# Handing out a Fourier layer over fewer tiles of a dense loop, and moving its loads and stores between queues

## The chip, the cores and the metric

The kernel runs on one core of a Trainium2 chip. The metric is the device time of one run, in microseconds (us); less is better. The core has five engines, each of which takes its instructions in the order in which they were written out: PE (TensorE, matmuls), DVE (VectorE), ACT (ScalarE), POOL (GpSimdE) and SP (SyncE, which here only issues DMA transfers). POOL and ACT can issue DMA transfers too.

## The reference

A Fourier layer over 8 sequences of 3008 steps by 256, then a gated two-layer network over each of the 24,064 rows, all in float32:

```
X = rfft(x, axis=1)                                   # (8, 1505, 256)
Yr = Xr @ w_r - Xi @ w_i + b_r ;  Yi = Xr @ w_i + Xi @ w_r + b_i
Yr, Yi = softshrink(Yr, 0.01), softshrink(Yi, 0.01)
y = irfft(Yr + 1j * Yi, n=3008, axis=1)               # (8, 3008, 256)
h = y @ w_in                                          # 256 -> 2048, w_in in float64
out = (h * cos(h)) @ w_out                            # 2048 -> 256, w_out in float64
```

## The kernel before

**The work.** The transform of length 3008 is a two-dimensional one of 64 by 47. A batch goes through three stages. Stage A (`stage_a`, line 379) loads x in 12 pieces xt (line 387), takes the transform of length 64 in 6 bursts of matmuls (pa) and stores the result by ao to a scratch array scr1 (line 403). Stage B (`stage_b`, line 409) loads it again as at (line 429), takes the transform of length 47 (pb, line 467), mixes the channels with the complex weights (`wmix`, pw, lines 514 to 516), shrinks, and takes the inverse of length 47 (`inverse`, pi). It goes through a batch in four quarters q = 0 to 3 of 8 frequencies. Stage C (`stage_c`, line 671) loads the result as bt (line 679) and takes the last inverse (pc, line 687) for one tile of 512 rows (the sixth: 448), which gives the dense network's input as a high and a low part, xTh and xTl.

For batches 1 to 7 a quarter ends so: VectorE forms st (lines 525 to 538), GpSimdE folds it (line 551 to 563), VectorE transposes it into tr, SP stores tr to a scratch array scrT in two halves (line 569) and loads it back as y in four pieces (line 576). `spread` (line 579) then has PE read y (pi) and SP store the result by bo to scr2 (line 592), from which bt is loaded. In batch 0, which runs alone at the start, `idft` (line 619) does this with a store at line 631.

**The dense network.** For each tile `moe_step` (line 718) runs 16 times: six matmuls ph (lines 725 to 727), four steps on ACT and DVE for h cos h, its high half gh on ACT, its low half gl on GpSimdE for every second step (line 267, called at line 738) or on DVE (line 270), and, three steps later, six matmuls po (`second`, lines 707 to 711). The weights' float64 words come in 16 pieces (raw, line 217) that are split in the start.

**What sets the order.** Batch b's dense work goes together with stage B of batch b + 1 and stage A of batch b + 2: the stages are generators that yield a cost, and `ahead` (line 796) is pulled twice in a dense step, at a rate that `share` (line 820) sets. `share` divides the cost of a batch's Fourier work by 6 - SPREAD tiles for batches 1 to 7, and by 5 - SPREAD_FIRST for batch 0. `stage_b` yields 5.0 ahead of its last inverse (line 665), to give y time. After the Fourier work, `ahead` yields a gap (GAP) and then stage C's first tile of the next batch. From this the framework's scheduler makes the final order of each engine when the program is built, by its own model of the time. The input tiles xt and at share one ring of six buffers (`stage_in`, line 320), so each load waits until PE has read what its buffer held. bt has one buffer, y one.

Of the kernel before, what the change touches and what calls it, by code (L numbers as in the profile page):

```python
# [38 lines left out]
GAP = 7  # L39
A_EVERY, A_FIRST = 5, 13  # L40
A_PAIR = 1.15
SPREAD, SPREAD_FIRST = 1.2, 1.1


def _r11(a):
# [95 lines left out]
def tile_body(ctx: ExitStack, tc, x, w_r, w_i, b_r, b_i, w_in, w_out,  # L141
              c_f2, c_sig, c_f3, c_ff, c_if, c_iw, c_sgn, out):
    nc = tc.nc
# [128 lines left out]
    scr1, scr2 = {}, {}  # L272
# [25 lines left out]
    def two(name):  # L298

        if "pro" not in pool:  # L300
            return [fps(name) for _ in range(2)]
        p = [ps.tile([128, 512], F32, tag=f"o{h}", name=name, bufs=1) for h in range(2)]
        side.extend((q, []) for q in p)
        return p
# [3 lines left out]
    def burst(calls):  # L308

        with tc.issue_after(mark["fill"].ins) if "pro" in pool else ExitStack():  # L310
            ins = mm(*calls[0][0], **calls[0][1])  # L311
        kept, n = (side, 3) if "pro" in pool else (ring, 4)
        if len(kept) >= n:
            for r in kept[-n][1]:
                behind(ins, r, "bank")
        with tc.high_priority(), tc.issue_after(ins.ins):
            for a, k in calls[1:]:
                mm(*a, **k)

    def stage_in(name):  # L320
        return wk.tile([128, 512], F32, tag="xt", name=name, bufs=6)

    def stage_out(name):
        return wk.tile([128, 1024], F32, tag="ao", name=name, bufs=3)
# [54 lines left out]
    def stage_a(b):  # L379
        scr1[b] = dr.tile([32, 2, 2, 24, 256], F32, tag="scr1", name=f"scr1_{b}")  # L380
        ld = {}

        def load(c):
            if c < 12:
                ld[c] = stage_in("xt")
                with tc.issue_after(mark["f0", 2].ins) if b == 1 else ExitStack():
                    nc.sync.dma_start(ld[c], x[b, :, 512 * c:512 * (c + 1)])

        for c in range(2):
            load(c)  # L390
        yield 0.0
        yield 1.0
        for cc in range(6):
            p = two("pa")
            xs = [ld.pop(2 * cc + v) for v in range(2)]
            burst([((p[h][64 * v:64 * v + 64], ff[64 * h:64 * h + 64, 256:], xs[v][64 * h:64 * h + 64]),
                    dict(start=True, stop=True, skip_group_check=True)) for h in range(2) for v in (1, 0)])
            ao = stage_out("ao")
            for h in range(2):
                drained(p[h], nc.scalar.copy(ao[:, 512 * h:512 * h + 512], p[h]))  # L400
            for v in range(2):
                i = 4 * cc + 2 * v
                nc.sync.dma_start(scr1[b][:, :, :, i:i + 2].rearrange("s r g i d -> (s r) g (i d)"),
                                  ao[64 * v:64 * v + 64].rearrange("p (g x) -> p g x", g=2))
                load(2 * cc + 2 + v)
            yield A_PAIR


    def stage_b(b):
        scr2[b] = dr.tile([48, 2, 32, 256], F32, tag="scr2", name=f"scr2_{b}")  # L410
        ld = {}
# [184 lines left out]
        def inverse(q):  # L596
            if b:
                yield from spread(q)
                return
            st = ST.pop(q)  # L600

            def t2(j):
                p = fps("pt")
                for sl in range(2):
                    for e in range(2):
                        o = sl * 256 + e * 128
                        nc.tensor.transpose(p[:96, o:o + 128],
                                            st[:, e, 2 * j + sl].rearrange("p r k -> p (r k)"), ident)
                y = pool["pro"].tile([128, 512], F32, tag="yf", name="yf", bufs=2)[:96]
                for sl in range(2):  # L610
                    ds = slice(256 * sl, 256 * sl + 256)
                    sc = sig[:, 8 * q + 2 * j + sl:8 * q + 2 * j + sl + 1]
                    if sl:
                        nc.vector.tensor_scalar(out=y[:, ds], in0=p[:96, ds], scalar1=sc, scalar2=None, op0=ALU.mult)
                    else:
                        nc.scalar.activation(y[:, ds], p[:96, ds], AF.Copy, scale=sc)
                Y[j] = y

            def idft(j):
                p = fps("pi")  # L620
                parts = ((0, 256, 0), (256, 512, 1)) if (q == 0 and j == 0) else ((0, 512, 1),)
                y = Y.pop(j)
                for lo, hi, v in parts:
                    ins = mm(p[:96, lo:hi], fi[0][:, v], y[:, lo:hi], start=lo == 0, stop=hi == 512,
                             skip_group_check=True)
                if q < 3:
                    mark["fill"] = ins
                bo = stage_out("bo")[:96, :512]
                nc.scalar.copy(bo, p[:96])
                s0 = 8 * q + 2 * j  # L630
                nc.sync.dma_start(scr2[b][:, :, s0:s0 + 2].rearrange("n r s d -> (n r) (s d)"), bo)

            t2(0)
            yield 0.43
            for j in range(4):
                if j < 3:
                    t2(j + 1)
                    yield 0.43
                else:
                    yield 0.8  # L640
                idft(j)
                yield 0.65
# [28 lines left out]
    def stage_c(b, t):  # L671
        th = pool["mo"].tile([128, 2, 512], F32R, tag="xTh", name="xTh", bufs=2)
        tl = pool["mo"].tile([128, 2, 512], F32R, tag="xTl", name="xTl", bufs=2)
        xT[b, t] = (th, tl)

        bt = wk.tile([128, 4, 256], F32, tag="bt", name="bt", bufs=1)
        for g in range(2):
            n0 = 24 * g + 4 * t
            nc.sync.dma_start(bt[64 * g:64 * g + 64],
                              scr2[b][n0:n0 + 4].rearrange("i r s d -> (r s) i d"))  # L680
        yield 3.5
        for hf in range(2):
            p = fps("pc")
            for j in range(2):
                for c in range(2):
                    o = 256 * j + 128 * c
                    ins = mm(p[:, o:o + 128], bt[:, 2 * hf + j, 128 * c:128 * c + 128], ff[:, 128:256], start=o == 0, stop=o == 384,  # L687
                             skip_group_check=True)
            mark.setdefault("pc", ins.ins)
            pv = p.rearrange("p (j c n) -> p c j n", j=2, c=2)  # L690
            thv, tlv = (a[:, :, 256 * hf:256 * hf + 256].rearrange("p c (j n) -> p c j n", j=2) for a in (th, tl))
            nc.scalar.copy(thv, pv)
            drained(p, nc.vector.tensor_tensor(out=tlv, in0=pv, in1=thv.bitcast(F32), op=ALU.subtract))
        yield 1.72
# [94 lines left out]
    for _ in stage_c(0, 0):  # L789
        pass  # L790
# [36 lines left out]
    for b in range(NB):  # L827
        fa = ahead(b)
        for t in range(NTT):
# [20 lines left out]
            while open_[0]:  # L850
                c = next(fa, None)
# [30 lines left out]
```

## Time and profile before

| | us |
|---|---|
| three runs: lowest, median, highest | 2718.5, 2720.4, 2724.3 |
| the profiled execution | 2718.7 |
| its span (first to last instruction) | 2716.9 |
| PE, DVE, ACT, POOL busy | 2656, 1786, 1676, 990 |
| mean granted clock of TensorE | 0.993 of 2.4 GHz |

A row of the profile names the line of the kernel, the engine, and what an instruction writes and reads (out<-in). Idle time of an engine stands in front of the instruction that ended it, with what released it. SPq is SP's queue of DMA issues; a DMA piece runs from its issue until its data has landed. One matmul of the program with plain float32 operands appears as two records. Fourier work of batch b stands beside dense work of batch b - 1, so "batch 2" below means the Fourier work of batch 2, from about 442 us to 770 us.

### The profile page before, as it was taken

How to read it: one execution, taken by the hardware profiler on the slowest of the kernel's cores; microseconds unless marked ns; L12 is line 12 of the kernel's file. 1: busy time of each engine (PE TensorE's matmuls, PEld its weight loads, DVE VectorE, ACT ScalarE, POOL GpSimd, SP SyncE). 2: the span in 40 equal slices, each digit the busy share in tenths (PEclk: the TensorE clock that was granted, in tenths of full speed). 3: DMA queues.
4: the chain of work that ended last, by engine and by line, in shares of the span. 5: the costliest groups of instructions: out<-in, count | busy, mean ns of one | idle time of the engine just before them, and what ended most of it. 6: DMA issues, size and time to landing. Idle time of an engine off the chain costs nothing.

```text
span 2716.9 us, 36600 instructions
## 1 busy us (share of the span) xinstructions
PE 2655.9 (98%) x13161; PEld 2181.1 (80%) x13161; DVE 1785.8 (66%) x2856; ACT 1676.3 (62%) x3020; POOL 989.7 (36%) x907
## 2 busy tenths in 40 slices
PE   8789999999999999999999999999999999999999
PEld 6468778888788887888878877788787888888888
DVE  6577765676657666676666666667665677656665
ACT  5566566656566665666566566665665666666666
POOL 4345432344314442244322544234332344422222
PEclk9899999999999999999999999999999999999999
DMA  6332343134311443124331234312433022211000
GB/s 194 112 110 83 106 119 84 56 98 133 99 48 46 127 119 90 54 65 114 100 103 44 70 106 114 96 41 77 123 104 85 31 82 84 75 43 31 16 16 15
DMA packets 148054, 224.92 MB, mean 83 GB/s; under 512 B 13840, under 2 KB 91168, under 8 KB 147872
## 3 DMA queue, kind: packets, MB, share of 16 engines
q1 hardware_dynamic: 142592, 205.24, 27.0%
q0 software_dynamic: 5280, 17.33, 2.1%
q8 instruction: 104, 1.70, 0.3%
q14 instruction: 78, 0.64, 0.1%
HBM read 121.33 MB, written 101.19 MB: 82 GB/s over the span
## 4 chain that ended last, share of the span: by engine, by line
PE 91%; DMA 3%; SPq 1%; ACT 0%; DVE 0%; issue 0%; POOL 0%; ACTq 0%; POOLq 0%; DVEq 0%
PE po L707 13%; PE po L711 12%; PE ph L725 12%; PE po L708 12%; PE ph L727 12%; PE ph L726 12%; PE pb L467 4%; PE pc L687 3%; PE pw L514 2%; PE pw L516 2%; PE pw L515 2%; PE pi L311 2%; DMA y<-scrT 2%; PE pa L311 1%; DMA bt<-scr 1%; DMA raw<-in_dram 0%
## 5 line engine op out<-in xcount | busy, mean ns | idle before, releaser
L267 POOL TENSOR_TENSOR gl<-u,gh 128x512 fp32r<-128x512 f32 (+1 forms) x384 | 490.6, 1278 | 1239.3 <-ACT gh L737 1003.5
L733 DVE SCALAR_TENSOR_TENSOR u<-ph,u 128x512 f32<-128x512 f32 (+1 forms) x768 | 520.0, 677 | 424.2 <-ACT u L732 419.3
L736 DVE TENSOR_TENSOR u<-ph,u 128x512 f32<-128x512 f32 (+1 forms) x768 | 519.0, 677 | 326.3 <-ACT u L735 312.9
L732 ACT ACTIVATE u<-ph 128x512 int32<-128x512 f32 (+1 forms) x768 | 452.8, 590 | 374.2 <-PE ph L727 364.4
L735 ACT ACTIVATE u<-u 128x512 f32<-128x512 f32 (+1 forms) x768 | 479.6, 625 | 321.5 <-DVE u L733 320.2
L725 PE MATMUL ph<-xTh,win 128*128 128x512 f32 (+1 forms) x1536 | 608.5, 396 | 5.6 <-DVE u L736 5.6
L707 PE MATMUL po<-gh,wout 128*128 128x512 f32 (+1 forms) x1536 | 599.6, 390 | 0.0
L726 PE MATMUL ph<-xTl,win 128*128 128x512 f32 (+1 forms) x1536 | 595.8, 388 | 0.0
L727 PE MATMUL ph<-xTh,win 128*128 128x512 f32 (+1 forms) x1536 | 595.3, 388 | 0.0
L708 PE MATMUL po<-gh,wout 128*128 128x512 f32 (+1 forms) x1536 | 594.9, 387 | 0.0
L737 ACT CAST gh<-u 128x512 fp32r<-128x512 f32 (+1 forms) x768 | 466.9, 609 | 205.4 <-DVE u L736 198.7
L711 PE MATMUL po<-gl,wout 128*128 128x512 f32 (+1 forms) x1536 | 481.7, 390 | 0.0
L270 DVE TENSOR_TENSOR gl<-u,gh 128x512 fp32r<-128x512 f32 (+1 forms) x384 | 309.2, 805 | 68.8 <-ACT gh L737 66.3
L725 PEld LDWEIGHTS ph<-xTh,win 128*128 128x128 f32 x1536 | 289.4, 188 | 74.6 <-issue 16.2
L707 PEld LDWEIGHTS po<-gh,wout 128*128 128x128 f32 x1536 | 289.0, 188 | 63.8 <-issue 11.4
L711 PEld LDWEIGHTS po<-gl,wout 128*128 128x128 f32 x1536 | 284.8, 188 | 67.7 <-POOL gl L267 8.1
L727 PEld LDWEIGHTS ph<-xTh,win 128*128 128x128 f32 x1536 | 288.9, 188 | 60.8 <-issue 6.1
L726 PEld LDWEIGHTS ph<-xTl,win 128*128 128x128 f32 x1536 | 289.4, 188 | 54.5 <-issue 6.5
L708 PEld LDWEIGHTS po<-gh,wout 128*128 128x128 f32 x1536 | 289.2, 188 | 52.7 <-issue 0.8
L551 POOL TENSOR_TENSOR st<-st,sgn 128x384 f32<-128x384 f32 x56 | 56.1, 1002 | 228.7 <-DVE st L538 228.7
L687 PEld LDWEIGHTS pc<-ff,bt 128*128 128x128 f32 x768 | 106.6, 196 | 24.8 <-issue 15.8
L467 PEld LDWEIGHTS pb<-f,at 96*128 96x128 f32 x896 | 116.6, 191 | 8.2 <-DVE tr L568 0.8
(115 smaller groups left out, 2573.5 us busy)
## 6 DMA issues: line engine op xcount, KB each, us to landing
scrT<-tr SPq DMA_DIRECT2D x56, 512.0 KB, 4.4
y<-scrT SPq DMA_DIRECT2D x112, 256.0 KB, 5.9
scr<-bo SPq DMA_DIRECT2D x128, 192.0 KB, 2.9
bt<-scr SPq DMA_DIRECT2D x96, 256.0 KB, 3.8
xt<-in_dram SPq DMA_DIRECT2D x84, 256.0 KB, 5.1
scr<-ao SPq DMA_DIRECT2D x84, 256.0 KB, 4.0
at<-scr SPq DMA_DIRECT2D x112, 192.0 KB, 3.0
out_dram<-ob SPq DMA_DIRECT2D x80, 256.0 KB, 2.2
```

The costliest lines, as they stand in the source:

```text
L267: return nc.gpsimd.tensor_tensor(out=lo, in0=x, in1=hi.bitcast(F32), op=ALU.subtract)
L707: mm(po[e][:, :n], wo[0][:, 0, f, es], gh[:, :n], start=f == 0, stop=False)
L708: mm(po[e][:, :n], wo[0][:, 1, f, es], gh[:, :n], start=False, stop=False)
L711: mm(po[e][:, :n], wo[0][:, 0, f, es], gl[:, :n], start=False, stop=f == NFC - 1)
L725: mm(h, win[:, 0, c, fs], th[:, c, :n], start=c == 0, stop=False)
L726: mm(h, win[:, 0, c, fs], tl[:, c, :n], start=False, stop=False)
L727: mm(h, win[:, 1, c, fs], th[:, c, :n], start=False, stop=c == 1)
L732: nc.scalar.activation(k[:, :n], h, AF.Identity, bias=0.25, scale=1.0 / TWO_PI)
L733: nc.vector.scalar_tensor_tensor(out=u[:, :n], in0=h, scalar=1.0 / TWO_PI, in1=k[:, :n], op0=ALU.mult, op1=ALU.subtract)
L735: nc.scalar.activation(u[:, :n], u[:, :n], AF.Sin, bias=HALF_PI, scale=TWO_PI)
L736: nc.vector.tensor_tensor(out=u[:, :n], in0=h, in1=u[:, :n], op=ALU.mult)
L737: nc.scalar.copy(gh[:, :n], u[:, :n])
```

## The change

Four edits. SPREAD goes from 1.2 to 1.6, so the Fourier work of a batch is shared out over 4.4 tiles and no longer 4.8; SPREAD_FIRST from 1.1 to 1.4, so that of batch 1, beside the dense work of batch 0, goes over 3.6 tiles and no longer 3.9. The loads of x for batches 2 to 7 (72 of 84) are issued by GpSimdE, those of batch 1 still by SP. The last four stores of batch 0's inverse (its fourth quarter) and the two loads of the first stage C are issued by ScalarE.

```diff
@@ -39,7 +39,7 @@
 GAP = 7
 A_EVERY, A_FIRST = 5, 13
 A_PAIR = 1.15
-SPREAD, SPREAD_FIRST = 1.2, 1.1
+SPREAD, SPREAD_FIRST = 1.6, 1.4
 
 
 def _r11(a):
@@ -384,7 +384,7 @@
             if c < 12:
                 ld[c] = stage_in("xt")
                 with tc.issue_after(mark["f0", 2].ins) if b == 1 else ExitStack():
-                    nc.sync.dma_start(ld[c], x[b, :, 512 * c:512 * (c + 1)])
+                    (nc.sync if b == 1 else nc.gpsimd).dma_start(ld[c], x[b, :, 512 * c:512 * (c + 1)])
 
         for c in range(2):
             load(c)
@@ -628,7 +628,7 @@
                 bo = stage_out("bo")[:96, :512]
                 nc.scalar.copy(bo, p[:96])
                 s0 = 8 * q + 2 * j
-                nc.sync.dma_start(scr2[b][:, :, s0:s0 + 2].rearrange("n r s d -> (n r) (s d)"), bo)
+                (nc.scalar if q == 3 else nc.sync).dma_start(scr2[b][:, :, s0:s0 + 2].rearrange("n r s d -> (n r) (s d)"), bo)
 
             t2(0)
             yield 0.43
@@ -676,8 +676,8 @@
         bt = wk.tile([128, 4, 256], F32, tag="bt", name="bt", bufs=1)
         for g in range(2):
             n0 = 24 * g + 4 * t
-            nc.sync.dma_start(bt[64 * g:64 * g + 64],
-                              scr2[b][n0:n0 + 4].rearrange("i r s d -> (r s) i d"))
+            (nc.scalar if b == 0 and t == 0 else nc.sync).dma_start(
+                              bt[64 * g:64 * g + 64], scr2[b][n0:n0 + 4].rearrange("i r s d -> (r s) i d"))
         yield 3.5
         for hf in range(2):
             p = fps("pc")
```

The new numbers set a new order on all engines. The places below show it.

PE, around the last inverse of batch 2 (pi reads y; ph and po are dense steps, their xTh names the tile). Before:

```order
L726 MATMUL ph_6700<-xTl_5824,win_82 128x512
L727 MATMUL ph_6700<-xTh_5823,win_82 128x512
L725 MATMUL ph_6700<-xTh_5823,win_82 128x512
L726 MATMUL ph_6700<-xTl_5824,win_82 128x512
L311 MATMUL pi_6689<-y_6596,iw_68 64x512
L318 MATMUL pi_6689<-y_6596,iw_68 64x512
```

After:

```order
L711 MATMUL po0_6527<-gl_6456,wout_1056 128x512
L711 MATMUL po1_6528<-gl_6456,wout_1056 128x512
L725 MATMUL ph_6579<-xTh_5913,win_82 128x512
L726 MATMUL ph_6579<-xTl_5914,win_82 128x512
L311 MATMUL pi_6535<-y_6327,iw_68 64x512
L318 MATMUL pi_6535<-y_6327,iw_68 64x512
```

The last matmul of the quarter's mixing (pw) stands 81 rows ahead of the first pi before, in the same tile (xTh_5823), and 117 rows ahead of it after, one tile earlier (xTh_5328); the pc rows of a tile now lie between the two.

SP's queue at the same place (scrT and y belong to the last quarter of batch 2, scr_3 and at to stage A and B of batch 3, scr_2 to batch 2's result). Before:

```order
L569 DMA scrT_3_6324<-tr 128x1024
L592 DMA scr_2_4317<-bo 96x1x512 x4
L716 DMA out_dram<-ob 128x512 x2
L403 DMA scr_3_4563<-ao 128x1x512 x2
L569 DMA scrT_3_6324<-tr 128x1024
L429 DMA at<-scr_3_4563 96x2x256 x4
L576 DMA y<-scrT_3_6324 32x8x256 x4
L429 DMA at<-scr_3_4563 96x2x256 x2
L592 DMA scr_2_4317<-bo 96x1x512 x4
L679 DMA bt<-scr_2_4317 64x4x256 x2
```

After:

```order
L569 DMA scrT_3_6198<-tr 128x1024
L592 DMA scr_2_4301<-bo 96x1x512 x4
L569 DMA scrT_3_6198<-tr 128x1024
L403 DMA scr_3_4541<-ao 128x1x512 x2
L576 DMA y<-scrT_3_6198 32x8x256 x4
L429 DMA at<-scr_3_4541 96x2x256 x6
L716 DMA out_dram<-ob 128x512 x2
L592 DMA scr_2_4301<-bo 96x1x512 x4
L679 DMA bt<-scr_2_4301 64x4x256 x4
```

Four loads of at stood between the second store to scrT and the loads of y; now two stores of stage A do, and the loads of at follow. In batch 1 it is the other way round: after the change five loads of at stand there.

GpSimdE, in the stretch where batch 4's first two pieces of x are loaded, after the change (f2 is a table for stage B, gl the dense steps' low halves):

```order
L267 TENSOR_TENSOR gl_7121<-u_7119,gh_7120 128x448
L387 DMA xt_7556<-in_0_dram 128x512
L267 TENSOR_TENSOR gl_7165<-u_7163,gh_7164 128x448
L267 TENSOR_TENSOR gl_7209<-u_7207,gh_7208 128x512
L387 DMA xt_7558<-in_0_dram 128x512
L455 DMA f2_7874<-in_7_dram 96x384
L267 TENSOR_TENSOR gl_7258<-u_7256,gh_7257 128x512
```

The two L387 rows stood in SP's queue before; here each waits for a matmul of pb that frees its buffer, with the next gl behind it.

ScalarE, at the end of batch 0's inverse (the rows with + are new there, those with - gone):

```order
-L629 COPY bo<-pi 96x512 x2
+L631 DMA scr_0_206<-bo 96x512
+L629 COPY bo<-pi 96x512
+L631 DMA scr_0_206<-bo 96x512
+L629 COPY bo<-pi 96x512
 L400 COPY ao<-pa 128x512 x2
 L238 CAST wout<-wa 128x512
-L400 COPY ao<-pa 128x512 x2
+L631 DMA scr_0_206<-bo 96x512
+L679 DMA bt<-scr_0_206 64x4x256
+L400 COPY ao<-pa 128x512
+L679 DMA bt<-scr_0_206 64x4x256
```

The last store and the two loads of bt now stand between the evacuations of stage A (L400) and the split of w_out (L238).

## Rows read from the trace of the kernel before

**Rows 1.** The page, busy time of PE: us, share of the span, instructions.

```profile
PE 2655.9 (98%) x13161; PEld 2181.1 (80%) x13161; DVE 1785.8 (66%) x2856; ACT 1676.3 (62%) x3020; POOL 989.7 (36%) x907
```

**Rows 2.** Waits of PE: who, for what: total us, times, longest us.

```profile
PE pi L311 <- DMA y<-scrT: 14.4, 6, 3.4
...
PE pc L687 <- DMA bt<-scr: 13.5, 4, 9.2
```

**Rows 3.** Stretches: us, busy us by engine (PE first), PEclk, DMA share, GB/s.

```profile
460.00:700.00 240.00, 240.00 (x1211) 199.30 (x1213) 162.97 (x263) 146.63 (x265) 100.05 (x94) 1.00 0.31 86
...
745.00:757.00 12.00, 9.21 (x39) 6.00 (x40) 3.36 (x5) 5.37 (x11) 1.26 (x1) 0.86 0.30 70
...
1405.00:1417.00 12.00, 9.31 (x47) 5.88 (x46) 4.89 (x8) 6.63 (x13) 1.26 (x1) 1.00 0.47 105
...
2062.00:2074.00 12.00, 9.16 (x40) 5.44 (x38) 4.06 (x7) 5.06 (x10) 1.26 (x1) 0.86 0.47 99
```

**Rows 4.** Order of time, PE, batch 2: start us, us, what, idle before.

```profile
725.30 0.34 PE L516 MATMUL pw<-Xl,wf 128*128 128x384 f32 x1
...
747.79 0.61 PE L311 MATMUL pi<-y,iw 55*64 55x512 f32 x1 [3.40 <-DMA y<-scrT]
...
749.28 0.63 PE L707 MATMUL po<-gh,wout 128*128 128x512 f32 x1
...
749.71 0.63 PE L708 MATMUL po<-gh,wout 128*128 128x512 f32 x1
```

**Rows 5.** Order of time, SP's queue, the same stretch.

```profile
732.41 0.61 SPq L569 DMA_DIRECT2D scrT<-tr  x1
...
735.97 2.47 SPq L429 DMA_DIRECT2D at<-scr  x4
...
738.54 1.87 SPq L576 DMA_DIRECT2D y<-scrT  x4
```

**Rows 6.** Order of time, PE, batch 1.

```profile
405.68 0.34 PE L516 MATMUL pw<-Xl,wf 128*128 128x384 f32 x1
...
423.18 0.61 PE L311 MATMUL pi<-y,iw 55*64 55x512 f32 x1 [0.23 <-DMA y<-scrT]
```

**Rows 7.** Order of time, SP's queue, batch 1.

```profile
414.76 2.09 SPq L576 DMA_DIRECT2D y<-scrT  x4
```

**Rows 8.** Order of time, PE, batch 7.

```profile
2351.80 0.34 PE L516 MATMUL pw<-Xl,wf 128*128 128x384 f32 x1
...
2374.09 0.64 PE L311 MATMUL pi<-y,iw 55*64 55x512 f32 x1
```

**Rows 9.** By line: ns min/median/max; wait of SP; last, landing of xt.

```profile
L455 POOL DMA_DIRECT2D f<-in_dram x56: 512/534/577, 19.3 to 2264.9; - x56
...
L217 POOL DMA_DIRECT2D raw<-in_dram x16: 527/722/772, 16.5 to 174.8; - x16
...
L267 POOL TENSOR_TENSOR gl<-u,gh x384: 1148/1292/1681, 149.2 to 2708.4; 128x512 fp32r<-128x512 f32 x160, 128x448 fp32r<-128x448 f32 x32
...
SPq L387 <- PE pa L318: 234.0, 13, 21.3
...
DMA to landing us min/median/max: 2.7/5.1/12.5
```

**Rows 10.** Groups by line: count, busy us, mean ns of one, idle before.

```profile
L496 POOL TENSOR_TENSOR Xl<-t,t 128x768 fp32r<-128x768 f32 x28 | 54.4, 1944 | 0.6
```

**Rows 11.** The start, SP's queue and PE; last, landing of bt.

```profile
118.70 0.81 SPq L679 DMA_DIRECT2D bt<-scr  x1
...
121.47 0.94 SPq L679 DMA_DIRECT2D bt<-scr  x1
...
130.11 1.19 PE L687 MATMUL pc<-ff,bt 128*128 128x128 f32 x4 [9.23 <-DMA bt<-scr]
...
DMA to landing us min/median/max: 3.3/3.8/8.5
```

**Rows 12.** The chain of waits: start us, us, what.

```profile
595.31 1.78 PE pc L687 x16
```

## Prediction

> **What bounds the kernel now.** I read the page's busy shares first, then the waits of PE, then the stretches, then the order of time around the longest waits. PE is busy for 98% of the span [rows 1], and in the stretch from 460 to 700 us it is busy for all 240 us at full clock [rows 3]: there nothing but fewer matmuls would help, and the change takes no matmul away. So the only time to be had lies in PE's waits. Two rows hold nearly all that is not part of the start [rows 2]: PE waits 14.4 us in 6 places for the load of y, and 13.5 us in 4 places for bt. The second is mostly one wait of 9.23 us before the first stage C [rows 11].
>
> The y waits are one pattern. In batch 2 the last matmul of the last mixing quarter (pw) starts at 725.30, and the inverse that reads y (pi) starts at 747.79 after 3.40 us of idle [rows 4]. Between them y's data goes through VectorE, GpSimdE, a store to scrT and a load back. That took 22.5 us, and PE had 19.1 us of other work (22.49 less 3.40). The waits before and after it are of the same kind; the first, in batch 1, is only 0.23 us [rows 6], so batches 2 to 6 share 14.2 us. Behind three of these five waits the clock falls to half: steps from one po matmul to the next are 0.43 us, from 749.28 to 749.71 [rows 4], in place of 0.23, which is 19.1 us over the 82 rows that the order has there, and a stretch of 12 us has a mean clock of 0.86 where another wait has 1.00 [rows 3]. That is 0.14 x 12 = 1.7 us of lost work each time, 5.0 us in all.
>
> **The change part by part.**
>
> *Handing out the Fourier work over 4.4 tiles.* The quarter's mixing ends sooner, and its inverse does not move up by as much. In the order, 81 rows of PE stand between the last pw and the first pi of batch 2, 77 of them MoE matmuls and 4 a burst of pa; in the changed kernel 117, of which 105 are MoE matmuls, 4 the burst and 8 are pc. Batches 3 to 6 have the same counts. 28 more MoE matmuls at 0.23 are 6.4 us, and the 8 pc rows (16 records in the trace) 1.8 us [rows 12]. PE then has 19.1 + 8.2 = 27.3 us of work for a path that took 22.5: 4.8 us to spare. The wait goes, and with it the fall of the clock: -14.2 - 5.0 us. What is late next is nothing on that path. The first pc behind the inverse keeps its place, 47 rows after it, where no bt wait stood in these batches. The second tile's pc moves from 36 rows behind the first to 26, which the last batch has now without a wait.
>
> Batch 1 is the weak spot. It goes from 73 rows to 78, but 20 of these are of the short last tile (448 columns of 512), so 17.3 us of work become about 17.9. Its path took 17.4 us (17.50 less the landing's few tenths) [rows 6], with y's load issued 9.1 us after the last pw [rows 6, 7]. Now five loads of at stand between the scrT store and y's loads on SP, as four did in batch 2, where 738.54 less 725.30 makes it 13.2 us [rows 5]. So y is late by between 0 (17.9 against 17.4) and 4.6 us (against 22.5). I take 2.0, somewhat nearer to batch 1's own path, whose batch it is; of the 0.2 us that it waited before nothing is gained. Batch 7 goes from 97 rows to 81: it had 22.3 us without a wait [rows 8] and now has 18.6. Its need is at most 22.3 and, by the lightest path seen, 17.4; I take no wait, with 0 to 3.7 us as bounds.
>
> *Loads of x by GpSimdE.* 72 loads leave SP's queue, where they stood waiting for their buffers for 234 us in 13 places alone [rows 9], and go to an engine that also makes the low halves gl. GpSimdE issues the f2 loads in 0.51 to 0.58 us and the larger raw loads in up to 0.77 us [rows 9], so the 72 cost it 37 to 55 us more, on an engine with 36% of the span busy. Each load waits there for the matmul that frees its buffer, and the next gl stands behind it. In the order, the closest reader of that next gl comes 31 matmuls after the releasing one, once; all others 37 or more. 31 matmuls are 7.1 us, and the load and one gl need 0.77 + 1.29 = 2.1 us [rows 9]. So I cost it at nothing: the cover is 5 us or more everywhere. It would cost PE the difference if an issue took over 5.8 us. The x data itself is read by PE 195 rows or more, over 40 us, after the matmul that lets its load go, against 12.5 us for the slowest landing of such a load [rows 9], so that is hidden too.
>
> On these loads the Trainium skill speaks against the change: "SBUF — State Buffer" (box on the "DVE blocks DMA" trap in "SBUF: two separate sides") says that a DMA issued by GpSimdE can't have its descriptors written while VectorE runs in a two-port mode, and gives some 3.1 us in place of 0.62. The f2 loads here, 56 of them, took at most 0.577 us, with VectorE busy for two thirds of the time [rows 3, 9]: so far the trace does not bear the rule out. What it would do is among the rivals.
>
> *ScalarE's stores and loads in the start.* Four stores and two loads move from SP to ScalarE. Before, the two halves of the first bt were issued at 118.70 and 121.47, the second behind a store of stage A, and PE started at 130.11 [rows 11]. On ScalarE they are not behind SP's x loads and stores, but ScalarE stands still until the last store of scr2 has landed, and what is queued behind it (evacuations ao of stage A, on which PE's pa waits, and a pass of the w_out split) comes later by that and by six issues of about 0.6 us, as the scrT store's [rows 5]. At best the second half lands 3.3 us after 121.5, the fastest landing of a bt load [rows 11], which is 5 us ahead of the start now; at worst the split and the evacuations are later by six issues, 4 us, and the weights for the first second() with them. I take 0: an earlier xT meets PE's next waits, which the weights set.
>
> *SPREAD_FIRST* moves work of batch 1 only, in stretches where PE is full: 0.
>
> Sum, against the profiled execution (2718.7 us, its span 2716.9): 2718.7 - 14.2 - 5.0 + 2.0 = 2701.5. The median of the three runs is 1.7 us above that execution, so half of it is added: **2702 us**.
>
> **Rivals.**
>
> *The wait moves (2710 us).* The inverse comes sooner and its followers with it: the load of bt for the second tile of a batch must land between two pc groups that now stand closer, and batch 1 and 7 wait in full. For it: the places named above. Against it: a bt load lands in a median of 3.8 us [rows 11] where 26 rows, 6 us, are left. Price: 4.6 - 2.0 more in batch 1, 3.7 in batch 7 and 0.4 in each of 5 batches: 8.3 us.
>
> *GpSimdE holds up PE (slower).* If a load of x stood in front of a gl whose reader is near, the wait of SP (234.0 us in 13, so 18 us each) would be GpSimdE's. From the point where the releasing matmul stands less than 2.1 us, 9 matmuls, before the reader of the next gl, each place costs PE what is missing; with 18 us against a lead of 7.1 us that is 11 us in 13 places, 143 us: 2845. The order speaks against it (31 is the smallest count). A smaller form, 72 loads that each add 0.5 us, gives 2738.
>
> *GpSimdE's issues are stretched by VectorE (2713 us).* In quarter 1 of each batch three issues stand ahead of the four adds that make Xl. From the last pb to the reader of Xl PE has 71 rows, 15.4 us; four adds of at most 1.94 us [rows 10] and a gl of 1.29 leave 6.3 us for the issues, and the first begins about 1 us before that pb is done: 2.4 us for each. If VectorE's work made an issue four times as long as the slowest of the trace (0.77 us), 3.1 us, three would be 2.1 us late in each of 5 batches: 11 us. Against it: 56 issues within 0.51 to 0.58 us. By the box in "SBUF — State Buffer" of the Trainium skill this is what would come, and its figure would give the same.
>
> *No change.* The scrT store or y's load is held by something other than distance, such as the stores of stage A that now stand between them on SP. Their pa burst is 18 rows, 4 us, behind the last pw, and the scrT store came 7.1 us after it (732.41) [rows 4, 5], so they are ready by then. The time would be 2718.
>
> **How the numbers follow.** Forecast 0.79; the wait moves 0.09; stretched issues 0.03; no change 0.05; held up 0.04. About 0.2% is what a measurement of this kernel can tell from no change, which is 2715. The forecast and the first rival lie below it, and most of the third: faster 0.90, same 0.06, slower 0.04. The range goes from 2718.7 - 19.2 - 5 (no wait in batch 1, the whole gain in the start), 2694, to the forecast with 2.6 in batch 1, 3.7 in batch 7 and 4 in the start, 2712; that leaves out about 1.5 in 10.
>
> **What would show it.** Right: no row of waits in which pi waits for y in batches 2 to 6, no half-clock stretch after 200 us, PE idle after 200 us of under 5 us, and gl's readers (L711) without waits for GpSimdE. Each of batches 2 to 6 becomes some 4 us shorter. In batch 1, y's wait shows what the five at loads cost. Wrong: PE waiting for GpSimdE or for Xl, issue times of xt on GpSimdE over 1 us, a bt wait in each batch, or a first stage C that starts after 134 us.

## The result, and the profile after

The changed kernel took 2690.2 us (median of three runs, before 2722.4 in the same comparison; ratio 0.988, 95% interval 0.9855 to 0.9905). Forecast were 2702 and a range from 2694 to 2712: the sign is right, the gain is larger than foreseen and the time lies outside the range. A fourth run took 6804.6 us, with 0.62 us from one dense matmul to the next in place of 0.23 (medians of its trace and of the one below), and one of *first_1_1* further down took 2920.0; both are left out. The trace below is from a second comparison (2694.2 against 2724.1; ratio 0.9885, 0.9872 to 0.9899).

First the busy time of PE on the page [rows 1], then its waits (total us, times, longest) [rows 2], then two stretches (columns as in [rows 3]):

```profile
PE 2655.4 (99%) x13161; PEld 2178.4 (81%) x13161; DVE 1791.7 (67%) x2856; ACT 1673.7 (62%) x3020; POOL 1031.5 (38%) x979
```

```profile
PE pc L687 <- DMA bt<-scr: 5.0, 3, 3.9
...
PE ph L725 <- DVE u L736: 3.2, 3, 1.4
...
PE pi L311 <- DMA y<-scrT: 1.1, 1, 1.1
```

```profile
718.00:730.00 12.00, 12.00 (x59) 8.11 (x58) 5.94 (x9) 8.54 (x16) 1.80 (x2) 1.00 0.16 40
...
130.00:165.00 35.00, 31.20 (x156) 23.32 (x157) 25.36 (x39) 22.92 (x43) 15.04 (x13) 0.94 0.73 210
```

The waits for y went from 14.4 us in 6 places to 1.1 in one. Around the last inverse of batch 2 (720.61) PE is now busy for all 12 us at full clock, where [rows 3] had 9.21 us at 0.86. And the waits for bt, nearly all in the start, went from 13.5 us to 5.0, which the forecast did not have.

PE in batch 1 and batch 2 (start us, us, what, idle before), to be read beside [rows 4, 6], and SP's queue there, beside [rows 5, 7]:

```profile
413.34 0.34 PE L516 MATMUL pw<-Xl,wf 128*128 128x384 f32 x1
432.41 0.61 PE L311 MATMUL pi<-y,iw 55*64 55x512 f32 x1 [1.13 <-DMA y<-scrT]
...
693.43 0.34 PE L516 MATMUL pw<-Xl,wf 128*128 128x384 f32 x1
...
720.61 0.64 PE L311 MATMUL pi<-y,iw 55*64 55x512 f32 x1
```

```profile
420.04 2.50 SPq L429 DMA_DIRECT2D at<-scr  x5
422.59 1.93 SPq L576 DMA_DIRECT2D y<-scrT  x4
...
699.88 0.33 SPq L569 DMA_DIRECT2D scrT<-tr  x1
700.36 1.19 SPq L403 DMA_DIRECT2D scr<-ao  x2
702.68 2.55 SPq L576 DMA_DIRECT2D y<-scrT  x4
706.08 2.89 SPq L429 DMA_DIRECT2D at<-scr  x6
```

In batch 2 the first pi comes 27.2 us after the last pw (720.61 less 693.43), as forecast (27.3), without a wait. y had landed after 17.5 us: its loads were issued 9.3 us after the last pw and no longer 13.2, and landed a little faster. In batches 3 to 6 the distance is 27.2 us too, and y landed after 17.8 to 19.3.

In batch 1 five loads of at now stand ahead of y's, and still y's are issued 9.25 us after the last pw (422.59 less 413.34; before 9.08). The waits of SP's queue show what had held them in batch 2: there the first load of at stood for stage A's stores (scr<-ao) to land. First before, from 725.3 to 740 us, then the changed kernel's batch 1, from 413.3 to 424 us:

```profile
SPq L429 <- DMA scr<-ao: 2.8, 1, 2.8
...
SPq L429 <- DMA scr<-ao: 0.2, 1, 0.2
```

The loads of x on GpSimdE (by line: count, ns min/median/max; then what GpSimdE waited for at them: total us, times, longest), beside [rows 9]:

```profile
L387 POOL DMA_DIRECT2D xt<-in_dram x72: 536/557/597, 177.6 to 1958.7; - x72
```

```profile
POOL xt L387 <- PE pb L467: 61.6, 34, 4.2
```

### The profile page after: what moved, and what is told of

Read it like the earlier page. It is cut to its first block, busy times and chain, and to the rows that moved or that the text cites. A ratio compares the mean times of both kernels' runs of the same rounds, so it can differ in the third digit from the quotient of the medians.

```text
span 6802.8 us, 36592 instructions
## 1 busy us (share of the span) xinstructions
PE 6790.0 (100%) x13161; PEld 4241.0 (62%) x13161; DVE 1763.7 (26%) x2856; ACT 1705.1 (25%) x3020; POOL 1008.1 (15%) x979
## 4 chain that ended last, share of the span: by engine, by line
PE 100%; DMA 0%; ACT 0%; DVE 0%; issue 0%; POOLq 0%
PE ph L727 13%; PE po L708 13%; PE ph L726 13%; PE ph L725 13%; PE po L711 13%; PE po L707 13%; PE pb L467 4%; PE pc L687 3%; PE pw L514 2%; PE pw L515 2%; PE pw L516 2%; PE pi L311 2%; PE pa L311 1%; PE pw L510 1%; PE pb L481 1%; PE pi L624 1%
## 5 line engine op out<-in xcount | busy, mean ns | idle before, releaser
L725 PE MATMUL ph<-xTh,win 128*128 128x512 f32 (+1 forms) x1536 | 1269.6, 827 | 0.0
L707 PE MATMUL po<-gh,wout 128*128 128x512 f32 (+1 forms) x1536 | 1258.2, 820 | 0.0
L708 PE MATMUL po<-gh,wout 128*128 128x512 f32 (+1 forms) x1536 | 1256.3, 818 | 0.0
L726 PE MATMUL ph<-xTl,win 128*128 128x512 f32 (+1 forms) x1536 | 1255.3, 817 | 0.0
L727 PE MATMUL ph<-xTh,win 128*128 128x512 f32 (+1 forms) x1536 | 1251.9, 815 | 0.0
L711 PE MATMUL po<-gl,wout 128*128 128x512 f32 (+1 forms) x1536 | 1088.6, 817 | 0.0
L708 PEld LDWEIGHTS po<-gh,wout 128*128 128x128 f32 x1536 | 544.1, 354 | 367.5 <-issue 363.8
L727 PEld LDWEIGHTS ph<-xTh,win 128*128 128x128 f32 x1536 | 534.5, 348 | 369.2 <-issue 359.0
L725 PEld LDWEIGHTS ph<-xTh,win 128*128 128x128 f32 x1536 | 543.0, 354 | 347.0 <-issue 291.6
L707 PEld LDWEIGHTS po<-gh,wout 128*128 128x128 f32 x1536 | 543.4, 354 | 343.8 <-issue 337.2
L711 PEld LDWEIGHTS po<-gl,wout 128*128 128x128 f32 x1536 | 538.4, 353 | 341.6 <-issue 281.0
L726 PEld LDWEIGHTS ph<-xTl,win 128*128 128x128 f32 x1536 | 550.8, 359 | 319.9 <-issue 316.6
L467 PEld LDWEIGHTS pb<-f,at 96*128 96x128 f32 x896 | 280.7, 423 | 47.5 <-issue 44.1
L467 PE MATMUL pb<-f,at 96*128 96x96 f32 x896 | 271.4, 523 | 0.0
```

Source lines behind the costliest of these rows:

```text
L467: mm(pv[:, j, :, c], at[:, j, 128 * c:128 * c + 128], f2[:, 2 * (hf % 2) + j], start=j == 0 and c == 0, stop=j == 1 and c == 1, skip_group ...
L707: mm(po[e][:, :n], wo[0][:, 0, f, es], gh[:, :n], start=f == 0, stop=False)
L708: mm(po[e][:, :n], wo[0][:, 1, f, es], gh[:, :n], start=False, stop=False)
L711: mm(po[e][:, :n], wo[0][:, 0, f, es], gl[:, :n], start=False, stop=f == NFC - 1)
L725: mm(h, win[:, 0, c, fs], th[:, c, :n], start=c == 0, stop=False)
L726: mm(h, win[:, 0, c, fs], tl[:, c, :n], start=False, stop=False)
```

## The experiments

All were compared with the kernel before in interleaved runs. A change in the median is given with the ratio and its interval. For the start, where two profiles differ by chance before anything changed, a second number is used, called *start* below: the us from PE's last matmul of batch 0's inverse (L624) to the 385th row of po, worked out from each trace. It is 273.2 in the trace of before and 261.4 in that of the changed kernel. Where the order is the same all through, it repeats to 0.3 us (272.9 in *spread_1_4*, 261.6 in *changed_2*), but *only_x*, whose order is that of before until 187 us, has 270.6, so 2 to 3 us of it say little about the first tens of us.

**The parts alone.** Each kernel is the one before with one part of the diff. *only_spread* has:

```diff
-SPREAD, SPREAD_FIRST = 1.2, 1.1
+SPREAD, SPREAD_FIRST = 1.6, 1.4
```

*only_act* has the two edits with `nc.scalar`, *only_x* the one with `nc.gpsimd`; *all_again* has all.

> The changed kernel itself once more, for a trace. The measured gain was about 30 us where 17 were forecast for the y waits and the clock behind them, so some 12 us more have to be found. Theory S (start): they are in the start; the first pc then begins at 118 to 121 us in place of 130.1, and PE's wait for bt goes from 13.5 us to under 4. Theory Q (queue): SP's queue, rid of the loads of x, issues everything of batches 2 to 7 earlier; the start is as before (first pc at 129 to 131 us), and each of batches 2 to 7 is 4 to 5 us shorter. Both expect no pi waiting for y in batches 2 to 6. In batch 1 the prediction expected a wait of 0 to 4.6 us for y.

> Before with SPREAD 1.6 and SPREAD_FIRST 1.4 alone; loads of x and the stores and loads of the start stay on SP. The prediction and theory S: the y waits of batches 2 to 6 and the half clock behind them go (-14.2 and -5.0, +0 to 4.6 in batch 1), the start stays: 2702 to 2705 us against 2722, first pc at 130 us. Theory Q: the loads of x on SP hold the rest of its queue, so y still waits 1 us or more in most batches: 2708 to 2715.

> Before with ScalarE issuing the last four stores of the first inverse and the two loads of the first stage C, and nothing else. Theory S: all of the missing 12 us: 2709 to 2712 against 2722, first pc at 118 to 121 us, the y waits as before (14.4 us in 6). Theory Q and the prediction's own term: 2718 to 2724, no difference.

> Before with the 72 loads of x for batches 2 to 7 issued by GpSimdE, and nothing else. The prediction: no difference, 2718 to 2724, PE not waiting for GpSimdE. Theory Q: 5 us or more faster (2710 to 2717), with y waits shorter than 14.4 us in sum. The rival of stretched issues: 10 us or more slower, with issues of xt of over 1 us on GpSimdE.

| | median us | ratio | interval |
|---|---|---|---|
| before | 2724.1 | | |
| all_again | 2694.2 | 0.9885 | 0.9872 to 0.9899 |
| only_spread | 2703.1 | 0.9915 | 0.9901 to 0.9928 |
| only_act | 2714.4 | 0.9956 | 0.9943 to 0.997 |
| only_x | 2725.5 | 1.0003 | 0.9994 to 1.0012 |

The parts add up: -21.0, -9.7 and +1.4 make -29.3, and all together gave -29.9. Theory Q falls, and theory S is right on the place, though not on its figures: the first pc starts at 127.9 us in *only_act* and at 129.9 with all parts, and not at 118 to 121. The waits of PE in *only_act*:

```profile
PE pi L311 <- DMA y<-scrT: 17.2, 6, 4.3
PE pc L687 <- DMA bt<-scr: 5.5, 3, 3.8
...
PE ph L725 <- DVE u L736: 2.7, 3, 1.4
```

But theory S put the gain on the first pc alone, and there PE waited only 5.4 us less than before (3.8 against 9.2), in a kernel whose *start* is shorter by 9.9 us (263.3). The stretch from 130 to 165 us, of before and then of *only_act*, shows where the rest was:

```profile
130.00:165.00 35.00, 26.04 (x118) 18.48 (x119) 20.32 (x36) 19.80 (x37) 12.50 (x12) 0.83 0.55 156
```

```profile
130.00:165.00 35.00, 30.85 (x157) 22.75 (x157) 25.65 (x41) 23.95 (x45) 16.45 (x15) 0.97 0.72 192
```

There are 39 more matmuls in the same 35 us, at 0.23 us each 9.0 us: PE was busy for 4.8 us more, and the clock was 0.97 in place of 0.83, which is another 4.9 us of 35. Some of this is the earlier first pc, which lies 2.1 us ahead of this stretch in *only_act* and at its beginning before. Counted in each trace from its own first pc to the 385th row of po, *only_act* takes 251.7 us and before 257.4; the first pc itself comes 11.6 us after the last matmul of the inverse and no longer 15.8. So some 5.8 of the 9.9 us lie behind the first pc.

**Stores or loads.** *stores_only* has only the first line below, *loads_only* only the second.

```diff
+                (nc.scalar if q == 3 else nc.sync).dma_start(scr2[b][:, :, s0:s0 + 2].rearrange("n r s d -> (n r) (s d)"), bo)
...
+            (nc.scalar if b == 0 and t == 0 else nc.sync).dma_start(
```

> Before with the last four stores of the first inverse on ScalarE, but the two loads of the first stage C still on SP. In ScalarE's order this kernel has what the changed kernel has: the first evacuations of ph (L732) stand ahead of the split's steps L236 and L238, where before has them behind these. Theory L (landing): ScalarE's edit gained 9.7 us because bt lands earlier, and all waits behind it shrink with it; here bt stays behind the loads of x and the stores of stage A, so 0 to 3 us. Theory O (order): 3.4 us come from bt, the other 6 from ScalarE's order; here about 6 us faster (2718 against 2724), PE's waits for u shrink from 5.6 us to some 3, the first pc stays at 15 us behind the last matmul of the first inverse.

> Before with the two loads of the first stage C on ScalarE, but the last four stores of the first inverse still on SP. ScalarE's order is that of before (ph's first evacuation behind L236 and L238). Theory L: 7 to 10 us faster, as with both. Theory O: 3 to 4 us faster, the first pc some 3 us earlier, and the waits of ph for u as before (5 to 6 us).

*stores_only*: 2716.0 against 2723.4 (0.9968, 0.9957 to 0.9979), *start* 266.5. *loads_only*: 2722.2 (0.9998, 0.9988 to 1.0008), *start* 271.0. Theory L falls: with the loads on ScalarE the first pc came as early as in *only_act* (11.5 us after the inverse), but from there to the 385th row of po it takes 259.5 us, 2.1 more than before, with a longer wait for bt in the third pc and a lower clock (0.79 in place of 0.84 over the 35 us from the first pc). The third pc of before, then PE in *loads_only*:

```profile
159.23 3.18 PE L687 MATMUL pc<-ff,bt 128*128 128x128 f32 x14 [3.00 <-DMA bt<-scr]
```

```profile
127.08 3.75 PE L687 MATMUL pc<-ff,bt 128*128 128x128 f32 x16 [3.56 <-DMA bt<-scr]
...
143.75 0.50 PE L725 MATMUL ph<-xTh,win 128*128 128x512 f32 x1 [2.69 <-DVE u L736]
...
158.07 2.72 PE L687 MATMUL pc<-ff,bt 128*128 128x128 f32 x14 [3.69 <-DMA bt<-scr]
```

Alone the loads show no gain. Beside the stores it is less clear: *only_act* and *stores_only* have the same order on PE, VectorE and GpSimdE, and *only_act* has the shorter *start* by 3.2 us, but by the ratios the 2 to 3 us between the two are within the intervals.

What the stores changed is read on ScalarE, first before, then *stores_only*:

```profile
140.06 0.67 ACT L229 ACTIVATE wm<-raw 128x512 f32<-128x512 f32 x1 [3.56 <-DMA raw<-in_dram]
...
141.68 0.70 ACT L236 ACTIVATE wm<-raw 128x512 f32<-128x512 uint32 x1 [0.95 <-DVE wq L231]
142.41 0.62 ACT L238 CAST wout<-wa 128x512 fp32r<-128x512 f32 x1
142.94 0.59 ACT L732 ACTIVATE u<-ph 128x512 int32<-128x512 f32 x1
...
147.94 0.66 ACT L229 ACTIVATE wm<-raw 128x512 f32<-128x512 f32 x1 [2.05 <-DMA raw<-in_dram]
...
149.54 0.57 ACT L400 COPY ao<-pa 128x512 f32<-128x512 f32 x1
```

```profile
141.74 0.69 ACT L229 ACTIVATE wm<-raw 128x512 f32<-128x512 f32 x1 [3.79 <-DMA raw<-in_dram]
142.32 1.06 ACT L732 ACTIVATE u<-ph 128x512 int32<-128x512 f32 x2
...
146.26 0.59 ACT L400 COPY ao<-pa 128x512 f32<-128x512 f32 x1
...
150.15 0.67 ACT L229 ACTIVATE wm<-raw 128x512 f32<-128x512 f32 x1 [0.29 <-DMA raw<-in_dram]
```

Before, the first evacuation of ph stands behind three steps of the weights' split, one of which waits for raw data and one for VectorE, and the evacuations ao stand behind the next wait for raw data. Behind ao stand SP's stores of stage A, and behind these the second half of the third bt. With the stores on ScalarE the scheduler wrote both the other way round.

**The order alone.** Three kernels leave every DMA on its engine and queue only steps of the split behind steps of the dense network, with edges that order an engine's instructions and make none wait. *order_only*, on ScalarE:

```diff
+        with behind_step("gh", 5):
+            nc.scalar.activation(m, v.bitcast(F32), AF.Abs)
...
+        with behind_step("sin", 4):
+            nc.scalar.activation(m, pair[:, :, 0], AF.Copy, scale=2.0 ** -52)
```

*order_only_2* does it for the twelfth and thirteenth piece, L238 included; *order_only_3* adds VectorE and SP:

```diff
+        with behind_step({11: ("mul", 0)}):
+            ve.tensor_scalar(out=qu, in0=mu, scalar1=0x07FFFFFF, scalar2=3,
...
+        if b == 0 and t == 2:
+            for i in sto[-4:-2]:
+                tc.add_manual_dep(i.ins, ld.ins.name, mybir.DependencyInfo(
```

*stores_old_order* is *stores_only* with the first ph's evacuation put back behind L238, and the first gh and two ao behind L229 of the next piece.

> Before with no DMA moved: from the fifth dense step on, the first step of a piece of the weights' split (L229 of before, which waits for its raw data) is issued by ScalarE behind the high half gh of five steps before, and its second one (L236) behind the sine of four steps before. So the evacuations ao of stage A and the steps of the dense layer stand ahead of it in ScalarE's order, as they do where ScalarE issues the four stores. Theory O (order): the gain of the stores was the new order of ScalarE, so 5 to 9 us faster than before; the third pc's wait for bt goes from 3.0 us to under 1, PE's waits for u from 5.6 us to 2 to 3.5; the first wait for bt stays at 8 to 10 us. Rival P: what counted were the stores themselves, off SP's queue: 0 to 2 us.

> Before with no DMA moved and ScalarE's order made more like that of the kernel with the four stores: the second and third step of the twelfth piece of the split (L236, L238 of before) behind the sine of the first and of the second dense step, the first step of the thirteenth piece (L229) behind the high half gh of the second. Theory O (order): 5 to 8 us faster than before, since the first evacuation of ph and the evacuations ao no longer stand behind steps that wait for VectorE or for raw data. Rival P (the stores themselves, off SP's queue): 0 to 3 us.

> The kernel with the four stores on ScalarE alone, with ScalarE's old order put back: the first evacuation of ph behind L238 of the twelfth piece, the first gh and two evacuations ao behind L229 of the thirteenth, which waits for its raw data. Theory O: the gain of the stores (7 to 9 us) goes, 2721 to 2726 against 2724; the third pc waits 3 us or more for bt again. Rival P: as with the stores alone, 2715 to 2717.

> As order_only_2, and the twelfth piece's steps on VectorE as well (L231 and L233 of before behind the first steps L733 of the first two dense steps, L235 behind the first L736), and SP issues the fourth pair of stage A's stores behind the loads of the third bt. So ScalarE, VectorE and SP have nearly the order of the kernel with the four stores on ScalarE, with no DMA moved between engines. Theory O (the order on all three): 6 to 9 us faster than before, the third pc and the first ph each wait under 1.5 us. Rival P (the stores themselves): 3 to 4 us, as order_only and order_only_2.

| | median us | before | ratio | interval | *start* |
|---|---|---|---|---|---|
| order_only | 2721.0 | 2723.9 | 0.9988 | 0.9979 to 0.9997 | 270.2 |
| order_only_2 | 2720.0 | 2724.7 | 0.9986 | 0.9977 to 0.9995 | 270.9 |
| order_only_3 | 2719.8 | 2724.0 | 0.9982 | 0.9973 to 0.9991 | 269.4 |
| stores_old_order | 2722.4 | 2724.7 | 0.9988 | 0.9979 to 0.9997 | 270.3 |

From both sides the order is worth about half of the stores' gain or somewhat more: order alone gains 3 to 5 us, and taking it back costs 5 of 7 to 9, each with an interval of 2 to 3 us to either side. The *start* of these four says no more, since *only_x* has 270.6 too (ScalarE of *stores_old_order*, whose line numbers are later by 7 to 14):

```profile
143.40 0.68 ACT L236 ACTIVATE wm<-raw 128x512 f32<-128x512 f32 x1 [3.79 <-DMA raw<-in_dram]
145.03 0.70 ACT L247 ACTIVATE wm<-raw 128x512 f32<-128x512 uint32 x1 [0.95 <-DVE wq L242]
...
146.28 1.56 ACT L746 ACTIVATE u<-ph 128x512 int32<-128x512 f32 x3
...
151.73 0.68 ACT L236 ACTIVATE wm<-raw 128x512 f32<-128x512 f32 x1 [1.85 <-DMA raw<-in_dram]
152.31 1.05 ACT L413 COPY ao<-pa 128x512 f32<-128x512 f32 x2
```

The 6 to 9 us that theory O expected of *order_only_3* did not come. In its trace ScalarE stands once more for raw data (L237 is before's L229), with two ao behind it:

```profile
156.90 0.67 ACT L237 ACTIVATE wm<-raw 128x512 f32<-128x512 f32 x1 [3.04 <-DMA raw<-in_dram]
...
158.47 1.07 ACT L413 COPY ao<-pa 128x512 f32<-128x512 f32 x2
```

So the order that was put in by hand isn't that of *stores_only* further on. PE's order differs from that of *stores_only* too, from 140 us on. Whether the other 3 to 5 us are the order further on, or the stores themselves, is open.

**The wait for raw data.** *two_raw_before* and *two_raw_after* give the raw weights a second buffer (that of Xh, in turn with that of y), before and in the changed kernel:

```diff
-            raw = wk.tile([128, 1024], U32, tag="y", name="raw", bufs=1)
+            raw = wk.tile([128, 1024], U32, tag=("y", "Xh")[len(raws) % 2], name="raw", bufs=1)
```

> Before with the raw weights in two buffers (those of y and of Xh in turn) in place of one: the next piece is loaded while the one before is split. Theory O says that ScalarE stood 3.6 and 2.1 us for raw data with evacuations queued behind it; here it doesn't stand, so 5 us or more faster than before, waits of PE for u under 3 us. If only the place in the order counts and not the wait for the data: 0 to 2 us.

> The changed kernel with the raw weights in two buffers. In its trace PE still waits 3.2 us for u, 0.9 us for xTh and 5.0 us for bt in the start. If ScalarE's standing for raw data is still a part of this: 2 to 4 us faster than the changed kernel (2690 against 2693); if not, the same.

*two_raw_before*: 2716.4 against 2723.9 (0.9974, 0.9965 to 0.9983), *start* 264.9. *two_raw_after*: 2688.2 (0.987, 0.9855 to 0.9886). In 125 to 165 us ScalarE's and PE's waits of before, and then what PE waited for in *two_raw_before*:

```profile
ACT wm L229 <- DMA raw<-in_dram: 13.4, 4, 6.6
...
PE ph L725 <- DVE u L736: 5.6, 2, 3.1
```

```profile
PE pc L687 <- DMA bt<-scr: 10.3, 2, 8.7
PE po L707 <- ACT ao L400: 1.5, 1, 1.5
PE ph L725 <- DVE u L736: 1.1, 1, 1.1
```

ScalarE has no wait for raw data left there, PE's waits for u fall from 5.6 us to 1.1, and the time falls by as much as with the four stores, with no DMA moved to another engine. Evacuations still stand behind L229 there; what is gone is its wait. But the second buffer also gave a new order, on ScalarE from 95 us on, so it is not shown how much of these 7 us is the wait for raw data and how much the order.

The version with both was run once more, beside the changed kernel (*changed_2*: 2691.4 us, 0.9884, 0.987 to 0.9897):

> The changed kernel with two raw buffers again, beside the changed kernel on the same chip. From the first look: 2 to 5 us faster than it, a ratio to before of 0.987 against 0.9885.

It took 2687.6 us (0.9863, 0.9848 to 0.9878). Its eight runs lie from 2683.3 to 2690.6, the four of *changed_2* from 2691.2 to 2693.1: it is the fastest version here, by 3.8 us in this comparison, though the intervals overlap (the changed kernel's first runs took 2690.0 to 2690.7).

**The loads of x with the new spread.** *spread_and_act* is the changed kernel with `nc.sync` for all loads of x.

> The changed kernel with the loads of x of batches 2 to 7 back on SP. The loads of x by GpSimdE alone gave nothing; with the new spread, y of batches 2 to 6 landed 22 us after the last pw with these loads on SP and 17.5 to 19.3 with them on GpSimdE, against 28.1 and 27.2 us of PE's work, so both are covered. Expected by that: the same time as the changed kernel within 2 us (about 2694). If the loads of x help the spread through SP's queue: 4 us or more slower than the changed kernel (2698 or more).

2692.7 against 2723.4 (0.9883, 0.9869 to 0.9896): the loads of x are worth nothing here either. In *only_spread* y landed 21.8 to 22.4 us after the last pw in batches 2 to 6, with GpSimdE's loads 17.5 to 19.3; both are under the 27 to 28 us of PE's work.

**Half of the spread.** *spread_1_4* is before with SPREAD 1.4.

> Before with SPREAD 1.4, half of the way to 1.6, and nothing else. Theory D (distance): what counts is how many rows of PE stand between the last pw and the first pi, and that is 75 here against 81 before and 121 with SPREAD 1.6 alone, since the pc of the next tile stay ahead of the last pw. 75 rows are 17.5 us against a path of 21 to 22.4 us: waits of 3.5 to 5 us in batches 2 to 6, 4 to 10 us slower than before. The rival (fewer tiles by themselves): about half of the 21 us of SPREAD 1.6, 2713.

2716.8 against 2723.4 (0.9975, 0.9966 to 0.9984): 7 us faster, where theory D had 4 to 10 slower. The distance did fall (to 17.7 us of PE's work), but the path fell with it. SP's queue in batch 2, and PE's waits:

```profile
718.92 0.33 SPq L569 DMA_DIRECT2D scrT<-tr  x1
719.47 1.19 SPq L403 DMA_DIRECT2D scr<-ao  x2
721.68 2.07 SPq L576 DMA_DIRECT2D y<-scrT  x4
```

```profile
PE pb L467 <- DMA at<-scr: 4.9, 5, 1.4
...
PE pi L311 <- DMA y<-scrT: 3.2, 5, 0.9
```

The loads of at no longer stand ahead of y's, which lands after 17.6 to 18.5 us in place of 21 to 22.4; now pb waits for at.

**SPREAD_FIRST.** *first_1_1* is the changed kernel with SPREAD_FIRST 1.1.

> The changed kernel with SPREAD_FIRST back at 1.1. The prediction's term for it was 0 in itself. By distance, batch 1 has 71 rows ahead of its last inverse in place of 78, so y's wait there becomes about 1.1 + 1.6 = 2.7 us: 1 to 2 us slower than the changed kernel, with the start unchanged. Rival: SPREAD_FIRST carries some 3 us of the gain elsewhere in batch 1: 3 to 5 us slower.

2692.5 (0.989, 0.9871 to 0.9909), y's wait in batch 1 0.50 us: neither the longer wait nor a gain elsewhere shows.

## Why the prediction was wrong, point by point

*The spread (predicted -14.2 - 5.0 + 2.0 = -17.2 us): right.* The count of rows gave the distance to 0.1 us (27.2 against 27.3). The waits of batches 2 to 6 and the half clock behind them are gone. Batch 1 waited 1.13 us where 2.0 was taken: its 78 rows took 17.9 us (19.07 less 1.13), as forecast (17.9), and its path 19.0, between the two bounds. The reason given for the 2.0 did not hold, though: the five loads of at delayed the issue of y by 0.2 us, since stage A's stores had landed by then. With the old order batch 1 waits 0.16 to 1.54 us too, from trace to trace (*order_only_2*, *loads_only*). Batch 7 had 18.8 us, forecast 18.6, and no wait. Alone it measured -21.0 us, or by the interval 19.6 to 27. By the traces of before and *only_spread*, counted from the last matmul of the first inverse to the end, it is -17.0 (2602.5 and 2585.5 us). The trace of before, from which the sum is taken, is of an execution of 2718.7 us, 5.4 under the median of that comparison, and among the lightest of the traces with the old spread: with 14.4 us of waits for y and 5 us of half clock. *only_act* has 17.2 us of waits, and around them 8.4 us of half clock (0.28 + 0.14 + 0.28 of 12 us each):

```profile
738.00:750.00 12.00, 9.18 (x35) 5.30 (x35) 2.78 (x5) 3.95 (x9) 1.26 (x1) 0.72 0.31 69
1070.00:1082.00 12.00, 9.20 (x39) 6.00 (x40) 3.37 (x5) 5.50 (x11) 1.26 (x1) 0.86 0.31 73
...
1730.00:1742.00 12.00, 8.91 (x30) 5.55 (x34) 2.13 (x4) 3.33 (x7) 1.19 (x1) 0.72 0.31 66
```

So the mechanism was right and its size somewhat low. One more reason given was not quite right. I took the path as fixed (22.5 us). With the spread alone it stayed at 21.8 to 22.4, but in the changed kernel it was 17.5 to 19.3, since it depends on what stands ahead of y on SP and on what that waits for. *spread_1_4* shows that this can count for as much as the distance.

*Loads of x by GpSimdE (predicted 0): right*, 1.0003 alone. The issues took 0.536 to 0.597 us, 61.6 us of waits for buffers stand on GpSimdE where SP had 234 [rows 9], and PE waited for no gl of GpSimdE. VectorE was busy for 67% of the span. From issue to landing these 72 loads took 3.0 to 8.4 us, 4.4 in the median, where SP's took 2.7 to 8.8, 3.5 in the median. The Trainium skill gives some 3100 ns in place of 620 for a DMA issued by GpSimdE that runs beside a VectorE `tensor_copy` ("SBUF — State Buffer", "A bandwidth-pool intuition that's wrong", under the box on the "DVE blocks DMA" trap). It gives this for the DMA as a whole; the prediction took it for the issue alone. Neither was stretched like that here, the issue to 0.597 us at most and the landing by a quarter in the median. No row tells whether VectorE ran an operation of that kind beside them, so this trace doesn't test the rule.

*ScalarE's stores and loads (predicted 0, with -5 and +4 as bounds): this step failed.* It measured -9.7 us, by the interval 8.2 to 15.5. Of the 12.1 us between the sum (-17.2) and the parts (-29.3) it is most; the spread gave 3.8 more than its term, and the loads of x took 1.4. "An earlier xT meets PE's next waits, which the weights set" was half right. The earlier bt did meet them: the loads, for whose sake I set the bound of -5, gave nothing alone. But the next waits were not fixed. They hung in part on evacuations that stood behind steps of the split in ScalarE's order, and these change places when the stores change engines; about half of the stores' gain is shown to be that, and the rest is open. I read ScalarE's order only as far as the moved DMAs, some ten rows, and the decisive rows stand behind them. The bound was wrong in the same way: it held the first wait of bt only, while the profile showed 3.0 us for the third bt, 5.6 for u, and a clock of 0.83 over 35 us (6 us) behind it, all within reach of the same change. The costs I feared did not show: the six issues took 0.31 to 0.98 us each on ScalarE.

*SPREAD_FIRST (predicted 0): right* within what *first_1_1* can tell.

*The rivals.* The wait moved nowhere: after 200 us PE waits for bt once, 0.74 us. GpSimdE held up nothing, nor were its issues stretched. What was missing among them is a gain in the start above 5 us.

## What to carry to other kernels

A distance in instructions times the step of the bounding engine tells well when a dependent matmul will come, but the path that it must cover depends on the queue ahead of its DMA and on what that queue waits for, so look at both in the new order. Where a scheduler writes the order, moving one DMA to another engine can reorder evacuations some twenty instructions on: compare the order of every engine until it runs alike again, and bound the step by all waits and low-clock time behind it, not by the first. An in-order engine that waits for a load holds up all that is queued behind it; here a second buffer for that load was worth as much as moving stores between queues (7.5 and 7.3 us).

## What the runs showed of the hardware

Waits for y of up to 0.93 us in *spread_1_4* left the granted clock of every 330 us stretch after 440 us at 1.00 in the profile, where the waits of 2.8 to 3.4 us of before had brought stretches of 12 us down to 0.86 [rows 3]. The length of a wait alone does not tell between these: behind one of 2.44 us in *order_only_3* the 12 us from 1733 have 0.86, behind one of 2.86 us in *only_act* those from 2062 have 1.00. And kernels whose instructions are the same up to the last matmul of the first inverse reach it between 114.3 us (before) and 118.4 (*order_only_2*): profiles of single executions can't be compared in the start by absolute times.
